# Folding eight logit columns into w_out, and native fp32 value products for eight pairs of heads instead of twelve

## The chip, the cores and the metric

The kernel runs on one core of one Trainium2 chip. The core has TensorE (PE in the rows; PEld is its loading of stationary operands), VectorE (DVE), ScalarE (ACT), GpSimd (POOL) and the queue engine SyncE (SP), which here only issues transfers. What is measured is the device time of one execution in microseconds (us). The number to predict is the median of several runs.

## The reference

Three layers follow each other, all in float32:

```python
# attention: 4 batches, 8 heads, 576 tokens, 64 columns per head
scores = q @ k.T / 8
scores = where(scores >= max(scores) - tau, scores, -1e9)
attn   = exp(scores - max) / (sum + 1e-9)
x      = (attn @ v), heads side by side          # 2304 tokens x 512
# first MoE: 512 -> 768 -> 512
h = maximum(maximum(x @ w1, x @ w2), x @ w3)
x = h @ w_out
# second MoE: one of 8 experts for each token
logits = x @ w_gate + modality_bias[modality_id]
e      = argmax(logits);  g = softmax(logits)[e]
out    = g * (relu(x @ w1[e]) @ w2[e])           # 512 -> 1024 -> 512
```

The logits are a linear function of h, since `x @ w_gate` is `h @ (w_out @ w_gate)`.

## The kernel before, in words

**Split products.** Most products of TensorE use a rounded format (F32R). Each operand is split into a high part (rounded) and a low part (the rest), and three products (high by high, high by low, low by high) are summed in a bank of PSUM. For some heads the products are made in native fp32 instead, without a split: `nat_s` pairs of heads for the scores and `nat_a` = 12 pairs for the values (`av`, L346). There are 32 pairs, in the order batch, group, pair; group 0 of a batch has 256 tokens, group 1 has 320. A value product of a native head is `m<-th,vv 128*64` in the rows; one of a split head has `128*128` and also reads `tl`, the low part of the transposed weights of attention.

**Attention tiles.** `run_tiles` (L658) goes through 144 tiles of 128 rows: four for a pair of group 0, five for a pair of group 1. For each tile, the scores of the next tile are made (`s<-kk,qh`), VectorE takes the maxima (L275) and applies the mask (L270), ScalarE takes the exponential (L295), TensorE transposes the tile before (`pt<-idn,e`), and when a head is complete its values are multiplied. A native head copies the transposed tile once (L323). A split head copies it to `pc` (L318), rounds it to `th` (L325) and subtracts to `tl` (L748, VectorE); its values are also split (L239 ScalarE, L240 GpSimd).

**First MoE as filler.** When the four pairs of a group are done, blocks of 256 tokens become ready: after tiles 16, 36, 52, 72, 88, 108 and 124 one each, and two at the end. `fill` (L400) weaves the generator `moe1` (L415) into the tiles: each tile grants 900 + 900 units, and the generator yields 440 or 430 units after a few products. A block has 18 accumulations of 12 products with 256 columns (w1, w2, w3, with the maximum on VectorE, L439), and then for each half of its tokens 18 products with 512 columns (`m<-w,hh` and `m<-w,hl`), whose sum ScalarE copies to `x1` (L465) and SyncE stores to `xd` (L466). PSUM tiles named `m` come from a pool with two banks, which values, first MoE and logits share. What is left of the blocks at the end of attention runs in `phase2`, where the banks are named `ph2`, in program order.

**Logits.** After a block, `logits` (L472) transposes each 128 tokens of x1 with four products (`m<-idn,x`), copies them to `x1t` on VectorE (L481), multiplies with `wgs` (8 columns, eight records in the trace) and adds the bias (L486). It runs as a side task of `fill`. The last block has its own version, `last_logits` (L490, L504 to L511). The routing of the second MoE reads the sums: `route_part`, `early` (which takes the most frequent expert of the first 16 token tiles as the early slot) and `final`.

**Weights.** `convert_weights` (L120) takes w1, w2, w3 and then w_out in 24 chunks of 512 columns from float64 words: a load, then one step on ScalarE (L138), three on VectorE (L139, L141, L143), a rounded copy on ScalarE (L144) and a subtraction on GpSimd (L145). `conv_step` makes at most three steps for each tile, so about one chunk a tile over the first 24 tiles; `convert` forces steps when a product needs a chunk that isn't there yet.

**Order.** The program's order is planned by the framework's timeline simulation when the kernel is built; in `phase2` TensorE's order is fixed by hand (`drive`), with due times in ns.

Of the kernel before, what the change touches and what calls it, by code (L numbers as in the profile page):

```python
# [10 lines left out]
F32 = mybir.dt.float32  # L11
F32R = mybir.dt.float32r
# [4 lines left out]
ALU = mybir.AluOpType  # L17
# [5 lines left out]
NT, DM, DFF = 2304, 512, 768  # L23
E, F2 = 8, 1024
# [8 lines left out]
G3 = 3  # L33
# [7 lines left out]
XROW = DM + 4  # L41
# [4 lines left out]
def f32(ap):  # L46
    return ap.bitcast(F32)


class Kern:  # L50
# [66 lines left out]
    def wtile(self):  # L117
        return self.wp.tile([128, WCH], F32R, name="w")

    def convert_weights(self):  # L120
        nc = self.nc
        nw = 3 * KF * KD * 128 // WCH
        self.wm = [(self.wtile(), self.wtile()) for _ in range(nw + KF * DM // WCH)]
        n = CCH
        for w, (hi, lo) in enumerate(self.wm):
            for s in range(WCH // n):
# [7 lines left out]
                hf, lf = hi[:, s * n:s * n + n], lo[:, s * n:s * n + n]  # L134
# [9 lines left out]
                nc.scalar.copy(hf, tf)  # L144
                nc.gpsimd.tensor_tensor(lf, tf, f32(hf), op=ALU.subtract)  # L145
                self.wready += n
                yield

    def w13s(self, f, m, kc):
        w, o = divmod(((f * 3 + m) * KD + kc) * 128, WCH)  # L150
        self.convert(w * WCH + o + 128)
        return [t[:, o:o + 128] for t in self.wm[w]]

    def wos(self, f):
        w, o = divmod(3 * KF * KD * 128 + f * DM, WCH)
        self.convert(w * WCH + o + DM)
        return [t[:, o:o + DM] for t in self.wm[w]]
# [257 lines left out]
    def moe1(self, i):  # L415
# [34 lines left out]
        x1s = self.x1s = []  # L450
        self.x1i = i
        for t in range(2):
            tt = 2 * i + t
            cs = slice(t * 128, t * 128 + 128)
            ps = self.psA()
            ops = []
            for f in range(KF):
                oh, ol = self.wos(f)
                ops += [(hH[f][:, cs], oh), (hL[f][:, cs], oh), (hH[f][:, cs], ol)]
            for n, (a, r) in enumerate(ops):  # L460
                self.mm(ps, lhsT=a, rhs=r, start=n == 0, stop=n == len(ops) - 1)
                if n % 2 and n < 17:
                    yield 430
            x1 = self.po.tile([128, DM], F32, name="x1")
            nc.scalar.copy(x1, ps)  # L465
            nc.sync.dma_start(self.xd[tt * 128:tt * 128 + 128, :], x1)  # L466
            x1s.append(x1)
            yield 430
        if i < NBLK - 1:
            self.side.append(self.logits(i, x1s))  # L470

    def logits(self, i, x1s):  # L472
        nc = self.nc
        for t in range(2):
            tt = 2 * i + t
            x1 = x1s[t]
            pt = self.psL()
            for kc in range(KD):
                self.tp(pt[:, kc, :], x1[:, kc * 128:kc * 128 + 128], self.idn)
            x1t = self.po.tile([128, KD, 128], F32, name="x1t", bufs=1)  # L480
            nc.vector.tensor_copy(x1t, pt)  # L481
            yield self.lag(440, 1500)
            pl = self.psL()[:, 0, :]
            for kc in range(KD):
                self.mm(pl[:, :E], lhsT=x1t[:, kc, :], rhs=self.wgs[:, kc, :], start=kc == 0, stop=kc == KD - 1)
            nc.vector.tensor_tensor(self.lg[:, tt, :], pl[:, :E], self.bias[:, tt, :], op=ALU.add)  # L486
            yield self.lag(440, 0)
        self.logged = i + 1

    def last_logits(self):  # L490
        nc = self.nc
        i = NBLK - 1
        xt = []
        pl = self.psL()
        for t in range(2):
            while len(self.x1s) <= t:
                yield 400
            yield 1100
            pt = self.psL()
            for kc in range(KD):  # L500
                self.tp(pt[:, kc, :], self.x1s[t][:, kc * 128:kc * 128 + 128], self.idn)
            xt.append(self.pa.tile([128, KD, 128], F32, name="x1t", bufs=2))
            if t:
                nc.scalar.copy(xt[t], pt)  # L504
            else:
                nc.vector.tensor_copy(xt[t], pt)
        for t in range(2):
            yield 1300 if t else 0
            for kc in range(KD):
                self.mm(pl[:, t, :E], lhsT=xt[t][:, kc, :], rhs=self.wgs[:, kc, :], start=kc == 0, stop=kc == KD - 1)  # L510
        nc.vector.tensor_tensor(self.lg[:, 2 * i:2 * i + 2, :], pl[:, :2, :E], self.bias[:, 2 * i:2 * i + 2, :], op=ALU.add)  # L511

    def phase1(self):
# [35 lines left out]
        self.conv = self.convert_weights()  # L549
# [3 lines left out]
    def phase2(self):  # L553
# [5 lines left out]
        self.psL = lambda: self.ps2.tile([128, DM], F32, name="y2p", bufs=G3).rearrange("p (a b) -> p a b", b=128)  # L559
# [6 lines left out]
                 (lambda: self.x1i == NBLK - 1, self.late_routing())]  # L566
# [140 lines left out]
    nat_a = 12  # L707
    x1s = ()
    x1i = -1
# [241 lines left out]
    def late_routing(self):  # L951


        for gen in (self.last_logits(), self.final()):
            while True:
                with self.tc.high_priority(offset=self.hot):
                    x = next(gen, None)
                if x is None:
                    break
                yield x  # L960
# [249 lines left out]
```

## Time and profile before

| | |
|---|---|
| median of 3 runs | 904.38 us (902.39 to 906.71) |
| profiled execution | 905.14 us, span 903.4 us |
| TensorE, VectorE, ScalarE, GpSimd busy | 859.1, 604.8, 565.5, 484.2 us |
| mean granted TensorE clock | 0.986 of full speed |
| attention tiles | 8.8 to about 590 us |
| first MoE | from about 68 to 682 us |
| slots of the second MoE | about 682 us to the end |

The span runs from the first to the last instruction of the profiled execution. Products are pipelined and their ends are modelled, so a busy time close to the span says that TensorE has work, not that it runs at its peak; start-to-start times tell what a product costs. The time in front of a row is its start in us, and x with a number is how many instructions the row merges.

### The profile page before, as it was taken

What the parts mean: (1) busy time and instruction counts of PE and PEld (TensorE: products, weight loads), DVE (VectorE), ACT (ScalarE), POOL (GpSimd) and SP (SyncE); (2) the same over time, 40 slices, a digit from 0 to 9 for tenths busy, and PEclk for the clock granted to TensorE, in tenths of its full rate; (3) what the DMA queues carried; (4) which work ended last, traced back from release to release, by engine and by line L of the source; (5) the groups of instructions that cost most, each with busy time, mean ns of one, the idle gap of its engine ahead of it and who ended that gap; (6) DMA issues with size and microseconds to landing.
All of it is one profiled execution on the core that took longest, in us unless ns stands there. A gap on an engine that the chain in (4) does not pass through costs nothing.

```text
span 903.4 us, 16815 instructions
## 1 busy us (share of the span) xinstructions
PE 859.1 (95%) x5616; PEld 761.9 (84%) x5616; DVE 604.8 (67%) x1425; ACT 565.5 (63%) x1167; POOL 484.2 (54%) x779
## 2 busy tenths in 40 slices
PE   7878999999999989999999999999999999999995
PEld 4546876787789979999988999989999899899894
DVE  6888984654488987887989889845475663453540
ACT  4767785665588897978998888741152353453440
POOL 5978996564576877967887877321030322121011
PEclk9988999999999999999999999999999999999998
DMA  6655652232222232332232221000050224320001
GB/s 185 173 151 151 165 151 65 80 85 60 68 74 58 79 99 60 87 94 59 74 91 73 81 86 54 9 24 1 27 220 24 71 58 152 117 71 36 1 36 37
DMA packets 58234, 74.26 MB, mean 82 GB/s; under 512 B 27424, under 2 KB 40480, under 8 KB 58144
## 3 DMA queue, kind: packets, MB, share of 16 engines
q1 hardware_dynamic: 54448, 63.66, 24.6%
q0 software_dynamic: 2880, 9.44, 3.1%
q8 instruction: 46, 0.75, 0.4%
q14 instruction: 44, 0.36, 0.1%
q10 hardware_dynamic: 816, 0.04, 0.1%
HBM read 80.46 MB, written 9.44 MB: 100 GB/s over the span
## 4 chain that ended last, share of the span: by engine, by line
PE 53%; issue 20%; DVE 8%; POOL 7%; ACT 6%; DMA 5%; SPq 0%; POOLq 0%; ACTq 0%; DVEq 0%
PE m L69 29%; PE ph L69 9%; PE s L69 6%; PE pt L72 4%; PE y2p L69 2%; POOL out L1153 2%; POOL kk L232 1%; DVE e L270 1%; DVE mx L275 1%; POOL xg L1075 1%; DVE tl L748 1%; PE p L72 1%; DMA tl<-w 1%; ACT e L295 1%; DMA qr<-q 1%
## 5 line engine op out<-in xcount | busy, mean ns | idle before, releaser
L69 PE MATMUL m<-xh,w 128*128 128x256 f32 x1008 | 202.3, 290 | 1.4 <-ACT xh L392 1.0
L69 PEld LDWEIGHTS m<-xh,w 128*128 128x128 f32 x1008 | 162.7, 192 | 5.3 <-issue 2.6
L69 PE MATMUL m<-xl,w 128*128 128x256 f32 x504 | 144.5, 287 | 2.4 <-POOL xl L393 2.3
L69 PE MATMUL m<-th,vv 128*64 128x256 f32 (+5 forms) x440 | 130.9, 381 | 8.7 <-ACT th L323 3.8
L270 DVE SCALAR_TENSOR_TENSOR e<-s,mx,e 128x576 f32<-128x576 f32 x144 | 116.8, 812 | 30.7 <-ACT e L295 29.0
L275 DVE TENSOR_REDUCE mx<-s 128x1 f32<-128x576 f32 x144 | 106.6, 750 | 33.8 <-PE s L69 32.9
L295 ACT ACTIVATE e<-s,mx 128x576 f32<-128x576 f32 x144 | 106.9, 743 | 17.4 <-DVE mx L275 12.6
L69 PE MATMUL ph<-x2h,w 128*128 128x384 f32 x384 | 103.8, 342 | 0.0
L69 PEld LDWEIGHTS m<-th,vv 128*64 128x64 f32 (+2 forms) x440 | 69.2, 167 | 39.5 <-issue 14.5
L69 PE MATMUL y2p<-w 128*128 128x512 f32 x432 | 100.5, 391 | 0.0
L69 PEld LDWEIGHTS m<-xl,w 128*128 128x128 f32 x504 | 96.5, 192 | 3.7 <-POOL xl L393 3.1
L69 PE MATMUL s<-kk,qh 128*128 128x288 f32 (+1 forms) x272 | 88.8, 357 | 11.3 <-DMA kk<-k 5.7
L232 POOL TENSOR_TENSOR kk<-kr,kk 64x576 fp32r<-64x576 f32 x60 | 90.3, 1505 | 16.3 <-ACT kk L231 6.4
L72 PE MATMUL pt<-idn,e 128*128 128x128 f32 x576 | 91.0, 279 | 6.4 <-ACT th L323 6.3
L69 PEld LDWEIGHTS y2p<-w 128*128 128x128 f32 x432 | 80.7, 188 | 16.3
L748 DVE TENSOR_TENSOR tl<-pc,th 128x512 fp32r<-128x512 f32 (+1 forms) x104 | 82.2, 798 | 10.4 <-ACT th L325 9.7
L1129 DVE SCALAR_TENSOR_TENSOR w<-ph,w 128x384 fp32r<-128x384 f32 x48 | 26.7, 556 | 82.7 <-ACT w L1128 82.5
L72 PEld LDWEIGHTS pt<-idn,e 128*128 128x128 f32 x576 | 69.9, 144 | 13.6 <-ACT th L323 8.8
L444 POOL TENSOR_TENSOR hl<-hacc,hh 128x256 fp32r<-128x256 f32 x54 | 44.1, 818 | 58.5 <-ACT hh L443 52.8
L69 PEld LDWEIGHTS s<-kk,qh 128*128 128x128 f32 (+1 forms) x272 | 53.6, 199 | 21.7 <-issue 9.2
L69 PEld LDWEIGHTS ph<-x2h,w 128*128 128x128 f32 x384 | 70.2, 188 | 0.2
L279 POOL TENSOR_SCALAR mx<-mx 128x1 f32<-128x1 f32 x144 | 40.9, 284 | 52.1 <-DVE e L270 36.8
(226 smaller groups left out, 2005.0 us busy)
## 6 DMA issues: line engine op xcount, KB each, us to landing
r<-w SPq DMA_DIRECT2D x48, 512.0 KB
kr<-k SPq DMA_DIRECT2D x120, 144.0 KB
tl<-w SPq DMA_DIRECT2D x18, 512.0 KB
qr<-q SPq DMA_DIRECT2D x120, 64.0 KB
vr<-v SPq DMA_DIRECT2D x40, 160.0 KB
xd<-x SPq DMA_DIRECT2D x18, 256.0 KB
vv<-v SPq DMA_DIRECT2D x24, 160.0 KB
tl<-wo SPq DMA_DIRECT2D x6, 512.0 KB
```

Of the source, the lines that this page charges most:

```text
L69: return self.pin(self.nc.tensor.matmul(*args, **kw))
L72: return self.pin(self.nc.tensor.transpose(*args, **kw))
L232: nc.gpsimd.tensor_tensor(kk[64:128], kr[64:128], f32(kk[64:128]), op=ALU.subtract)
L270: self.conv_step(v.scalar_tensor_tensor(e, sv, mx[:, 1:2], e, op0=ALU.is_ge, op1=ALU.mult, accum_out=mx[:, 2:3]))
L275: self.conv_step(v.tensor_reduce(mn[:, 0:1], sn, axis=AX.XY, op=ALU.max, negate=True))
L279: nc.gpsimd.tensor_scalar(mx[:, 3:4], mx[:, 2:3], 1e-9, None, op0=ALU.add)
L295: nc.scalar.activation(e, sv, AF.Exp, bias=mx[:, 0:1], scale=1.0)
L444: nc.gpsimd.tensor_tensor(l, acc[f], f32(h), op=ALU.subtract)
L748: nc.vector.tensor_tensor(l, src, f32(h), op=ALU.subtract)
L1075: self.nc.gpsimd.indirect_dma_start(out=xg, out_offset=None, in_=sl["src"], in_offset=bass.IndirectOffsetOnAxis(ap=sl["gidx"][:, g:g + 1], ...
L1129: nc.vector.scalar_tensor_tensor(h[:, SLOT:2 * SLOT], ph, 0.0, f32(h[:, :SLOT]), op0=ALU.max, op1=ALU.subtract)
L1153: nc.gpsimd.indirect_dma_start(out=sl["out"][g], out_offset=bass.IndirectOffsetOnAxis(ap=sl["sidx"][:, g:g + 1], axis=0), in_=y, in_offset ...
```

## The change

The eight columns of w_out times w_gate are made once, from the converted w_out, and stand beside the columns of w_out: each half of the token tile's output is then a product of 256 + 8 columns and one of 256. The eight columns of the sum get the bias and are the logits. `logits` and `last_logits` go away. For this, w_out is converted first and w1, w2, w3 after it, and each of the six chunks of w_out is transposed and multiplied with w_gate in two further steps (`gate_columns`) while the next chunk is converted. `moe1` yields 440 after four products and 220 after each half. The routing of the last block begins when its logits are there. Separately, `nat_a` becomes 8: pairs 8 to 11 (batch 1, group 0) use split value products.

```diff
--- before.py
+++ after.py
@@ -38,7 +38,8 @@
 NC = KF2 // 2
 NK = 6
 WBUF = 24
-XROW = DM + 4
+HALF = DM // 2
+ROW = DM + E
 WCH = 1024
 CCH = 512
 
@@ -114,15 +115,24 @@
 
         self.xd = self.ctx.enter_context(tc.tile_pool(name="dram", bufs=1, space=DRAM)).tile([NT, DM], F32, name="xd")
 
-    def wtile(self):
-        return self.wp.tile([128, WCH], F32R, name="w")
+    def wtile(self, full=False):
+        w = self.wp.tile([128, 2 * ROW], F32R, name="w")
+        return w if full else w[:, :WCH]
+
+    def conversion(self):
+        for _ in self.convert_weights():
+            if self.gates and next(self.gates[0], self) is self:
+                self.gates.pop(0)
+            yield
 
     def convert_weights(self):
         nc = self.nc
         nw = 3 * KF * KD * 128 // WCH
-        self.wm = [(self.wtile(), self.wtile()) for _ in range(nw + KF * DM // WCH)]
+        self.wm = [(self.wtile(w >= nw), self.wtile(w >= nw)) for w in range(nw + KF * DM // WCH)]
         n = CCH
-        for w, (hi, lo) in enumerate(self.wm):
+
+        for w in [*range(nw, len(self.wm)), *range(nw)]:
+            hi, lo = self.wm[w]
             for s in range(WCH // n):
                 src, c0 = (self.w13, w) if w < nw else (self.wo, w - nw)
                 c0 = c0 * WCH + s * n
@@ -131,7 +141,6 @@
                 t = self.po.tile([128, n], F32, name="x1").bitcast(U32)
                 nc.sync.dma_start(raw, src[:, c0:c0 + n].bitcast(U32).rearrange("p (c two) -> p c two", two=2))
                 h, l = raw[:, :, 1], raw[:, :, 0]
-                hf, lf = hi[:, s * n:s * n + n], lo[:, s * n:s * n + n]
                 tf = t.bitcast(F32)
 
 
@@ -141,20 +150,45 @@
                 nc.vector.scalar_tensor_tensor(t, h, 0x80000000, t, op0=ALU.bitwise_and, op1=ALU.bitwise_or)
                 yield
                 nc.vector.scalar_tensor_tensor(t, l, 29, t, op0=ALU.logical_shift_right, op1=ALU.bitwise_or)
-                nc.scalar.copy(hf, tf)
-                nc.gpsimd.tensor_tensor(lf, tf, f32(hf), op=ALU.subtract)
+                if w < nw:
+                    parts = [(s * n, 0, n)]
+                else:
+                    parts = [(s * ROW, 0, HALF), (s * ROW + HALF + E, HALF, HALF)]
+                for o, i, m in parts:
+                    hf = hi[:, o:o + m]
+                    nc.scalar.copy(hf, tf[:, i:i + m])
+                    nc.gpsimd.tensor_tensor(lo[:, o:o + m], tf[:, i:i + m], f32(hf), op=ALU.subtract)
+                if w >= nw:
+                    o = s * ROW + HALF
+                    self.gates.append(self.gate_columns(tf, hi[:, o:o + E], lo[:, o:o + E]))
                 self.wready += n
                 yield
 
+    def gate_columns(self, w, hi, lo):
+
+        nc = self.nc
+        yield
+        pt = self.psL()
+        for kc in range(KD):
+            self.tp(pt[:, kc, :], w[:, kc * 128:kc * 128 + 128], self.idn)
+        wt = self.pe.tile([128, 4, 128], F32, name="pc", bufs=2)
+        nc.scalar.copy(wt, pt)
+        yield
+        pl = self.psL()[:, 0, :E]
+        for kc in range(KD):
+            self.mm(pl, lhsT=wt[:, kc, :], rhs=self.wgs[:, kc, :], start=kc == 0, stop=kc == KD - 1)
+        self.split_out(hi, lo, pl)
+
     def w13s(self, f, m, kc):
         w, o = divmod(((f * 3 + m) * KD + kc) * 128, WCH)
-        self.convert(w * WCH + o + 128)
+        self.convert(KF * DM + w * WCH + o + 128)
         return [t[:, o:o + 128] for t in self.wm[w]]
 
     def wos(self, f):
-        w, o = divmod(3 * KF * KD * 128 + f * DM, WCH)
-        self.convert(w * WCH + o + DM)
-        return [t[:, o:o + DM] for t in self.wm[w]]
+
+        w = (3 * KF * KD * 128 + f * DM) // WCH
+        o = f % 2 * ROW
+        return [[t[:, a:b] for t in self.wm[w]] for a, b in ((o, o + HALF + E), (o + HALF + E, o + ROW))]
 
     def convert(self, n):
         while self.wready < n:
@@ -447,68 +481,27 @@
             if i == NBLK - 1 and self.eslot and n0 >= 6:
                 self.weights(n0 // 2)
             yield 440
-        x1s = self.x1s = []
-        self.x1i = i
         for t in range(2):
             tt = 2 * i + t
             cs = slice(t * 128, t * 128 + 128)
-            ps = self.psA()
-            ops = []
-            for f in range(KF):
-                oh, ol = self.wos(f)
-                ops += [(hH[f][:, cs], oh), (hL[f][:, cs], oh), (hH[f][:, cs], ol)]
-            for n, (a, r) in enumerate(ops):
-                self.mm(ps, lhsT=a, rhs=r, start=n == 0, stop=n == len(ops) - 1)
-                if n % 2 and n < 17:
-                    yield 430
             x1 = self.po.tile([128, DM], F32, name="x1")
-            nc.scalar.copy(x1, ps)
+            for d in range(2):
+                n = HALF + E * (1 - d)
+                ps = self.psA()[:, :n]
+                ops = []
+                for f in range(KF):
+                    oh, ol = self.wos(f)[d]
+                    ops += [(hH[f][:, cs], oh), (hL[f][:, cs], oh), (hH[f][:, cs], ol)]
+                for n, (a, r) in enumerate(ops):
+                    self.mm(ps, lhsT=a, rhs=r, start=n == 0, stop=n == len(ops) - 1)
+                    if n % 4 == 3:
+                        yield 440
+                nc.scalar.copy(x1[:, d * HALF:d * HALF + HALF], ps[:, :HALF])
+                if d == 0:
+                    nc.vector.tensor_tensor(self.lg[:, tt, :], ps[:, HALF:], self.bias[:, tt, :], op=ALU.add)
+                yield 220
             nc.sync.dma_start(self.xd[tt * 128:tt * 128 + 128, :], x1)
-            x1s.append(x1)
-            yield 430
-        if i < NBLK - 1:
-            self.side.append(self.logits(i, x1s))
-
-    def logits(self, i, x1s):
...
         self.logged = i + 1
-
-    def last_logits(self):
...
     def phase1(self):
         tc = self.tc
@@ -546,7 +539,8 @@
         self.ph = opn(p1, "ph", 1)
         self.po = opn(p1, "po", 2)
         self.wready = 0
-        self.conv = self.convert_weights()
+        self.gates = []
+        self.conv = self.conversion()
         self.run_tiles(heads, tiles)
         at.close()
 
@@ -556,14 +550,13 @@
         self.pa = opn(ctx, "p2a", 1, side="right")
         self.ps2 = opn(ctx, "ps2", 1, PSUM, side="right")
         self.raw = tuple(self.pa.tile([128, NC, WCH], F32, name=n) for n in ("r1", "r2"))
-        self.psL = lambda: self.ps2.tile([128, DM], F32, name="y2p", bufs=G3).rearrange("p (a b) -> p a b", b=128)
         self.psA = lambda: self.ps2.tile([128, 512], F32, name="ph2", bufs=3)
         self.outs = dram_disjoint_views(self.out, (NSTAT + 2) * G3)
         self.route_tiles()
         self.pinned = True
         self.slots = []
         parts = [(lambda: self.logged >= 7, self.route_part(0, 14)), (lambda: self.logged >= 8, self.early()),
-                 (lambda: self.x1i == NBLK - 1, self.late_routing())]
+                 (lambda: self.logged >= NBLK, self.late_routing())]
         self.drive(self.main(), parts)
         n = nc.values_load(self.eT[0:1, NTL:], min_val=NSTAT * G3, max_val=NTL)
         with tc.For_i(NSTAT * G3, n, G3) as i:
@@ -704,9 +697,7 @@
             self.prepped += 1
 
     nat_s = 2
-    nat_a = 12
-    x1s = ()
-    x1i = -1
+    nat_a = 8
     eslot = None
     conv_rate = (1, 1)
     conv_credit = 0
@@ -950,14 +941,13 @@
 
     def late_routing(self):
 
-
-        for gen in (self.last_logits(), self.final()):
-            while True:
-                with self.tc.high_priority(offset=self.hot):
-                    x = next(gen, None)
-                if x is None:
-                    break
-                yield x
+        gen = self.final()
+        while True:
+            with self.tc.high_priority(offset=self.hot):
+                x = next(gen, None)
+            if x is None:
+                break
+            yield x
 
     def final(self):
```

## Rows read from the trace of the kernel before

**Rows 1.** The page, busy time, share of the span and instructions.
```profile
PE 859.1 (95%) x5616; PEld 761.9 (84%) x5616; DVE 604.8 (67%) x1425; ACT 565.5 (63%) x1167; POOL 484.2 (54%) x779
```

**Rows 2.** Stages: length, PE, PEld, DVE, ACT, POOL busy, clock, DMA, GB/s.
```profile
0.00:100.00 100.00, 81.59 (x366) 52.40 (x367) 82.06 (x177) 68.93 (x135) 77.64 (x125) 0.93 0.59 163
...
162.50:231.00 68.50, 67.07 (x452) 54.15 (x451) 34.46 (x98) 43.17 (x97) 39.52 (x76) 1.00 0.27 70
...
375.40:515.00 139.60, 135.87 (x1016) 129.60 (x1015) 119.42 (x289) 118.31 (x263) 107.78 (x180) 0.99 0.28 78
...
600.00:727.00 127.00, 126.17 (x902) 118.51 (x901) 67.80 (x226) 36.58 (x68) 25.11 (x32) 1.00 0.19 67
```

**Rows 3.** TensorE's waits, 130 to 600 us: total, times, longest.
```profile
PE s L69 <- DVE e L270: 4.1, 6, 1.4
...
PE m L69 <- DVE x1t L481: 1.7, 2, 1.2
...
PE m L69 <- ACT xh L392: 0.2, 1, 0.2
```

**Rows 4.** Timeline of TensorE: first MoE, 256 columns (start, busy us).
```profile
578.82 0.40 PE L69 MATMUL m<-xh,w 128*128 128x256 f32 x2
579.06 0.28 PE L69 MATMUL m<-xl,w 128*128 128x256 f32 x1
```

**Rows 5.** Timeline of TensorE: w_out, 512 columns.
```profile
680.52 0.39 PE L69 MATMUL ph<-w,hl 128*128 128x512 f32 x1
680.75 0.61 PE L69 MATMUL ph<-w,hh 128*128 128x512 f32 x2
681.20 0.39 PE L69 MATMUL ph<-w,hl 128*128 128x512 f32 x1
```

**Rows 6.** Timeline of all engines: the last logits.
```profile
681.43 0.39 PE L69 MATMUL ph<-w,hh 128*128 128x512 f32 x1
...
683.25 0.60 PE L72 MATMUL y2p<-idn,x 128*128 128x128 f32 x4
683.68 0.96 PE L69 MATMUL y2p<-wgs,x1t 128*128 128x8 f32 x8
...
684.49 0.42 PE L69 MATMUL ph<-x2h,w 128*128 128x384 f32 x1
...
687.15 0.17 DVE L511 TENSOR_TENSOR bias<-y2p,bias 128x16 f32<-128x16 f32 x1 [0.77 <-PE y2p L69]
```

**Rows 7.** Timeline of TensorE: native values of one head.
```profile
201.52 2.51 PE L69 MATMUL m<-th,vv 128*64 128x256 f32 x10
203.96 0.40 PE L69 MATMUL s<-kk,qh 128*128 128x288 f32 x1
```

**Rows 8.** Groups by line, 313.5 to 375.4 us: busy, mean ns, idle before.
```profile
L748 DVE TENSOR_TENSOR tl<-pc,th 128x512 fp32r<-128x512 f32 x16 | 14.6, 918 | 1.2 <-ACT th L325 1.2
...
L318 ACT COPY pc<-pt 128x512 f32<-128x512 f32 x16 | 9.4, 585 | 0.5 <-DVE mx L275 0.4
...
L240 POOL TENSOR_TENSOR vv<-vr,vv 128x320 fp32r<-128x320 f32 x7 | 6.2, 881 | 1.8 <-ACT vv L239 1.5
...
L239 ACT CAST vv<-vr 128x320 fp32r<-128x320 f32 x8 | 3.7, 459 | 0.1
```

**Rows 9.** Timeline of ScalarE: exponentials of tiles 34, 36, 52, 72, 88.
```profile
159.16 0.75 ACT L295 ACTIVATE e<-s,mx 128x576 f32<-128x576 f32 x1
...
163.70 0.76 ACT L295 ACTIVATE e<-s,mx 128x576 f32<-128x576 f32 x1
...
230.96 0.74 ACT L295 ACTIVATE e<-s,mx 128x576 f32<-128x576 f32 x1
...
313.51 0.74 ACT L295 ACTIVATE e<-s,mx 128x576 f32<-128x576 f32 x1
...
375.40 0.74 ACT L295 ACTIVATE e<-s,mx 128x576 f32<-128x576 f32 x1
```

**Rows 10.** Groups by line, whole span: weight loads of the w_out products.
```profile
L69 PEld LDWEIGHTS m<-w,hh 128*128 128x128 f32 x156 | 29.1, 188 | 6.6 <-ACT remh L248 0.5 <-issue 0.4 <-DVE hacc L439 0.3
```

More of the change, by code (lines that the diff above doesn't have):

```diff
@@ L465, in moe1 @@
-            nc.scalar.copy(x1, ps)
-            nc.sync.dma_start(self.xd[tt * 128:tt * 128 + 128, :], x1)
-            x1s.append(x1)
-            yield 430
-        if i < NBLK - 1:
-            self.side.append(self.logits(i, x1s))
-    def logits(self, i, x1s):
[L473 to L487, printed above, removed]
-        self.logged = i + 1
@@ L490, in last_logits @@
-    def last_logits(self):
[L491 to L511, printed above, removed]
+            x1 = self.po.tile([128, DM], F32, name="x1")
```

## The prediction

> **What bounds the kernel now.** I read the page first: TensorE is busy for 859 of 903 us, VectorE for 605, ScalarE for 566, GpSimd for 484 [rows 1]. An average hides stages, so I split the span next [rows 2]. In the first 100 us VectorE is the fullest (82.1, against 81.6 of TensorE with a granted clock of 0.93): this is where the weights are converted. In the stretches shown from 162 to 515 us TensorE is at 97 to 98%, but VectorE and ScalarE are near 85% from 375 to 515 us; from 600 to 727 us TensorE has 126.2 of 127 us and the others little. Busy TensorE counts modelled ends, so I took the waits as a check: between 130 and 600 us the twelve groups of its waits sum to 14 us, the largest 4.1 us on VectorE's mask, and 1.7 us on the copy x1t of the logits [rows 3]. So after 130 us TensorE's stream sets the pace, and the change is to be priced in start-to-start times of products, not in their durations (a 256-column product lasts 0.28 us, but two start within 0.24 us).
>
> **Price of a column.** 256 columns: (579.06 - 578.82)/2 = 0.120 us from start to start [rows 4]. 512 columns: (681.20 - 680.52)/3 = 0.227 us [rows 5]. On the line between them 264 columns take 0.120 + 8 x 0.107/256 = 0.123 us.
>
> **The change part by part.**
>
> *The logits' own products go.* For each of 18 token tiles four transposes (683.25 to 683.68, 0.43 us) and eight product records with wgs (683.68 to 684.49, 0.81 us) go, 1.24 us [rows 6]: 18 x 1.24 = -22.3 us, 12 tiles (14.9 us) before 600 us and 6 (7.4 us) after. What TensorE waited for x1t goes too: -1.7 us [rows 3]. VectorE loses the copies x1t; its bias add stays.
>
> *w_out in two halves.* Each 512-column product becomes one of 264 and one of 256: 0.123 + 0.120 - 0.227 = +0.016 us; 9 blocks x 36 = 324 products: +5.3 us. Each half has its own weight load. That is in the prices, since the 256-column stream has a load for each product too. The Trainium skill puts it otherwise (TensorE: Matmul & The Clock Gate, Back-to-back issue gap): in a stream of load and product pairs it gives some 81 ns at 128 columns and 131 ns at 512; by that, drawn as a line, a half costs 98 ns and a pair 65 ns more than the whole, 21 us in all and not 5.3. The trace's 227 ns for 512 columns does not agree with it, so the rows decide.
>
> *Evacuation.* ScalarE copies two halves instead of 512 columns, and VectorE adds the eight logit columns from the same bank. That bank, one of two named m, now waits for both engines. The next half gives 18 x 0.12 = 2.2 us of cover in the other bank; VectorE's longest queue item is 0.8 us. I cost it at nothing; if VectorE lags by 3 us, it is 0.8 us for each of 18 tiles, 14 us.
>
> *Weights: w_out first, and gate columns.* Six chunks gain 4 transposes and 8 product records each: 6 x 1.24 = 7.4 us of TensorE, all in the first 100 us, where it has idle time and VectorE is the fullest [rows 2]. For VectorE it is six subtractions of 8 columns. GpSimd and ScalarE get two halves for one chunk, plus a copy of 512 columns on ScalarE. These are fractions of a microsecond a chunk on engines that the row of that stage shows less full than VectorE. New is a wait: the transposes wait for the converted chunk, and behind them on TensorE's queue stand the next tile's scores, for which VectorE's maxima wait. From 0 to +7.4 us (all products in the open); I take +2, since the chunk was finished one step earlier. That w13 comes six chunks later is hidden: the first block begins at tile 16, one chunk is converted for each tile, so ten are there, and the block needs about 1.4 for each tile and 18 in all; it never catches up.
>
> *Values of pairs 8 to 11.* A head's native product is 10 records in 2.44 us (201.52 to 203.96) [rows 7]; split it is 9 products of 256 columns, 1.08 us. Eight heads: at most -10.9 us. In exchange each head brings two copies pc (0.59 us) and one vv cast (0.46) to ScalarE, two tl of 0.92 us to VectorE, one vv of 0.88 us to GpSimd [rows 8]. There is room: in these tiles (162.5 to 231.0) VectorE is busy for 34 of 68 us, ScalarE for 43 [rows 2]. The best yardstick is the same kind of group that already runs split: 16 tiles took 230.96 - 163.70 = 67.3 us native, 375.40 - 313.51 = 61.9 us split, with the same grant to the first MoE for each [rows 9]. I take the difference, -5.4 us, which holds the new side work; bounds -10.9 and 0.
>
> *The filler budget.* Each tile grants 1800 to the first MoE. A block asked for 9 x 2640 + 2 x 3870 and 1760 for its logits, 33260; it will ask for 23760 + 2 x 3960 = 31680, so 17.6 tiles and not 18.5. Blocks become ready at fixed tiles (16, 36, 52, 72, 88, 108, 124). Before, only the first block ran out before the next was ready (tiles 34.5 to 36); after, four do, for 2.4 + 0.8 + 0.8 + 0.8 = 4.8 tiles, 3.3 more. The filler's part of a tile is 1800/31680 of a block's 216 x 0.120 + 72 x 0.122 = 34.7 us, 2.0 us. If a dry tile takes as long as a full one (67.3/16 = 4.2 us), these 2.0 us of TensorE are lost, 6.5 us in all. Tiles 34 and 35 took (163.70 - 159.16)/2 = 2.3 us each [rows 9], the full time less 1.9, by which nothing is lost. Two tiles are few, and each starts when the planned order lets it; I take the middle, +3. The rest of block 6 (18 products) moves ahead of 600 us, which is neutral where TensorE is full.
>
> *The end of the routing.* The last w_out product starts at 681.43 us and the last logits are added at 687.15 [rows 6]; after the change the add follows the product, some 5 us earlier. But the early slot's products cover the routing in any case: TensorE has work for 126.2 of 127 us there [rows 2]. Nothing gained.
>
> **Sum.** -22.3 - 1.7 + 5.3 + 2 - 5.4 + 3 = -19.1 us. The profiled execution took 905.1 us (its span 903.4), 0.7 over the median of 904.4: 905.1 - 19.1 - 0.7 = 885 us. The order of the instructions is planned anew, which no row prices; the range takes it.
>
> **Rivals.**
>
> *More lands.* The split values give all 10.9 us and dry tiles run faster: 905.1 - 22.3 - 1.7 + 5.3 + 2 - 10.9 = 877.5, range 870 to 880. For it: TensorE is the fullest in all those stages. Against: ScalarE, 43 us now and 8 x (2 x 0.59 + 0.46) = 13 us more, reaches 56/62 = 90% in pairs 8 to 11.
>
> *Half lands before 600 us.* VectorE and ScalarE, at 85%, take over the pace: 7.4 + 7.4 of the logits, 3 of the values: 905.1 - 14.8 - 3 + 5.3 + 2 + 3 = 898; range 891 to 900.
>
> *Nothing lands before 600 us.* Only 7.4 us less 72 x 0.016 = 1.2 after it: 905.1 - 6.2 + 2 + 3 = 904, no change. Against: the waits of [rows 3].
>
> *Slower: gate products in the way early.* Place: the first ten tiles, 12 stops (transposes, then products, six times) at the head of TensorE's queue, each waiting on VectorE's conversion or a free bank m. The other terms give 21 us, so from 21/12 = 1.8 us a stop the gain is gone, and from 2.2 us it is slower by 0.5%; at 3 us, 919. For it: VectorE is full there and three conversion steps lie between load and result. Against: TensorE has 18 idle us in that stage.
>
> *Slower: a load for each half stands in the open.* 324 more loads of some 0.188 us [rows 10] would be 61 us: 941. The 256-column stream with a load for each product at 0.120 us [rows 4] speaks against it. The skill's pace of pairs named above would give 901 instead, and the traces so far refute it at 512 columns.
>
> **Chances.** Forecast (880 to 891) 0.52; more 0.20; half 0.13; nothing 0.08; gate products 0.05; loads 0.02. A measurement here tells about 0.5% (4.5 us) from no change. Faster by more: the first two and most of the third, 0.83. Within: nothing, and the rest of half, 0.10. Slower: 0.07. The range takes in more and half: 871 to 899; it leaves out the last three cases and the edges.
>
> **What would show it.** Between 150 and 600 us no product with wgs and no copy x1t, and two halves starting 0.24 us apart together. The 16 tiles of pairs 8 to 11 in 62 us rather than 67, with ScalarE near 90%. The first 36 tiles ending (the exponential of tile 36) within 3 us of 163.7. Stretches without first-MoE products before tiles 36, 72, 108 and 144. From the end of attention to the first second-layer product of the early slot, some 10 us less, of which 4 are only moved. I am wrong if tiles 0 to 36 take over 5 us more, if TensorE waits on bank m (its releaser a VectorE bias or ScalarE copy) for over 5 us, or if pairs 8 to 11 keep their 67 us.

## The result and the profile after

The changed kernel takes 894.69 us (median of four runs, 889.62 to 895.52) against 903.76 us for the kernel before; the ratio is 0.987 (95% interval 0.9839 to 0.99). So it is faster by 1.3%, by 9 us and not by the 19 that I forecast. The profiled run took 895.52 us with a span of 893.7 us.

First the page, busy time by engine, as in [rows 1], and then the four stages of [rows 2], the middle two moved to where their tiles now stand (the second is now exactly tiles 36 to 52):

```profile
PE 842.5 (94%) x5788; PEld 766.4 (86%) x5788; DVE 609.8 (68%) x1447; ACT 580.0 (65%) x1226; POOL 492.3 (55%) x793
```

```profile
0.00:100.00 100.00, 79.77 (x320) 53.80 (x321) 68.48 (x150) 60.36 (x127) 64.32 (x114) 0.89 0.55 148
180.06:244.31 64.25, 59.22 (x453) 53.70 (x452) 47.73 (x118) 51.32 (x112) 48.19 (x79) 1.00 0.28 78
391.60:531.00 139.40, 134.85 (x1084) 131.35 (x1084) 117.77 (x291) 122.11 (x274) 108.61 (x186) 1.00 0.29 84
600.00:727.00 127.00, 125.92 (x957) 120.78 (x956) 71.63 (x235) 40.03 (x77) 28.71 (x34) 1.00 0.20 71
```

TensorE is busy for 17 us less in all, yet in the first 100 us every engine does less than before: VectorE, the fullest there, fell from 82 to 68 us. It isn't relieved; it waits. The exponentials of tiles 4, 16, 36, 52, 72 and 88 on ScalarE, the counterpart of [rows 9], show what that costs:

```profile
21.88 0.75 ACT L329 ACTIVATE e<-s,mx 128x576 f32<-128x576 f32 x1
88.83 0.74 ACT L329 ACTIVATE e<-s,mx 128x576 f32<-128x576 f32 x1
180.06 0.74 ACT L329 ACTIVATE e<-s,mx 128x576 f32<-128x576 f32 x1 [0.16 <-DVE mx L314]
244.31 0.72 ACT L329 ACTIVATE e<-s,mx 128x576 f32<-128x576 f32 x1
317.44 0.75 ACT L329 ACTIVATE e<-s,mx 128x576 f32<-128x576 f32 x1
383.46 0.75 ACT L329 ACTIVATE e<-s,mx 128x576 f32<-128x576 f32 x1
```

Cut at such exponentials, the two profiled spans differ like this (us):

| stretch | before | after | difference |
|---|---|---|---|
| start to tile 36 | 163.7 | 180.1 | +16.4 |
| tiles 36 to 52 (pairs 8 to 11) | 67.3 | 64.2 | -3.1 |
| tiles 52 to 143 | 357.3 | 342.3 | -15.0 |
| tile 143 to the end | 315.1 | 307.1 | -8.0 |

After tile 36 the change gives 26 us; the first 36 tiles take 16 of them back, 13 of these between tiles 4 and 16 (54.0 us before, 67.0 after).

**How they are lost.** Tiles 4 to 16, before and after, in the columns of [rows 2] (TensorE is the first busy time, VectorE the third):

```profile
20.76:74.80 54.04, 44.37 (x195) 26.41 (x194) 46.85 (x95) 40.02 (x79) 45.29 (x61) 0.91 0.58 162
```

```profile
21.88:88.83 66.95, 55.42 (x234) 37.95 (x232) 46.45 (x100) 42.99 (x95) 46.46 (x68) 0.85 0.47 132
```

VectorE has as much work as before, 46 us. TensorE is busy for 11 us more, but its idle time does not shrink: 9.7 us before, 11.5 after. The gate products, busy for 13.2 us there, were not taken up by the idle time; they came on top of it. Two places in those twelve tiles show how VectorE is kept waiting. Here is TensorE, then VectorE, around the first:

```profile
32.96 1.87 PE L70 MATMUL m<-wgs,pc 128*128 128x8 f32 x8
34.77 4.72 PE L70 MATMUL m<-th,vv 128*64 128x256 f32 x10
39.42 1.00 PE L73 MATMUL pt<-idn,e 128*128 128x128 f32 x4
40.39 0.38 PE L70 MATMUL s<-kk,qh 128*128 128x288 f32 x1
40.61 0.29 PE L70 MATMUL s<-kk,ql 128*128 128x288 f32 x1
```

```profile
36.10 0.17 DVE L334 TENSOR_TENSOR w<-m,w 128x8 fp32r<-128x8 f32 x1 [0.22 <-ACT w L333]
41.21 0.76 DVE L309 TENSOR_REDUCE mx<-s 128x1 f32<-128x576 f32 x1 [4.95 <-PE s L70]
```

A gate product, a head's native values and transposes run for 7.4 us ahead of the scores, and VectorE stands for 4.95 us. Besides, TensorE is at half its pace: the ten records take 4.72 us here and 2.51 us in [rows 7] (the last section tells how to read its clock there). At the second place VectorE itself is the cause:

```profile
70.43 0.82 DVE L304 SCALAR_TENSOR_TENSOR e<-s,mx,e 128x576 f32<-128x576 f32 x1 [0.30 <-ACT e L329]
...
74.74 0.43 DVE L148 TENSOR_SCALAR x<-x 128x512 uint32<-128x512 uint32 x1 [3.48 <-ACT x L147]
...
78.27 0.69 DVE L152 SCALAR_TENSOR_TENSOR x<-tl,x 128x512 uint32<-128x512 uint32 x1
78.88 0.75 DVE L309 TENSOR_REDUCE mx<-s 128x1 f32<-128x576 f32 x1
```

```profile
73.34 0.29 PE L70 MATMUL s<-kk,ql 128*128 128x288 f32 x1
```

```profile
73.97 0.66 ACT L147 ACTIVATE x<-tl 128x512 f32<-128x512 f32 x1 [2.76 <-DMA tl<-w]
```

The scores were done at 73.6 us, but their maxima stand in VectorE's queue behind two conversions, the first of which waits for ScalarE, which waits for a chunk's load; TensorE then has next to nothing to do until 81 us (0.34 us of work from 76 to 80). No gate product stands here: the last of them ended at 61 us. VectorE's waits for scores in tiles 4 to 16 add up to 10.8 us.

### The profile page after: what moved, and what is told of

It reads as the page before. It is cut to its first block, busy times and chain, and to the rows that moved or that the text cites. A ratio compares the mean times of both kernels' runs of the same rounds, so it can differ in the third digit from the quotient of the medians.

```text
span 893.7 us, 17267 instructions
## 1 busy us (share of the span) xinstructions
PE 842.5 (94%) x5788; PEld 766.4 (86%) x5788; DVE 609.8 (68%) x1447; ACT 580.0 (65%) x1226; POOL 492.3 (55%) x793
## 4 chain that ended last, share of the span: by engine, by line
PE 57%; issue 19%; POOL 8%; ACT 6%; DMA 5%; DVE 4%; SPq 1%; POOLq 0%; ACTq 0%; DVEq 0%
PE m L70 31%; PE ph L70 10%; PE s L70 7%; PE pt L73 5%; DMA kr<-k 3%; PE y2p L70 2%; POOL out L1143 2%; POOL kk L266 2%; POOL xg L1065 1%; PE p L73 1%; DMA tl<-w 1%; ACT e L329 1%; ACT kk L265 1%; DVE tl L739 1%; DVE mx L309 1%
## 5 line engine op out<-in xcount | busy, mean ns | idle before, releaser
L70 PE MATMUL m<-xh,w 128*128 128x256 f32 x1008 | 199.5, 287 | 6.0 <-DVE xf L406 2.1
L70 PEld LDWEIGHTS m<-xh,w 128*128 128x128 f32 x1008 | 160.6, 188 | 10.2 <-DVE xf L406 2.9
L304 DVE SCALAR_TENSOR_TENSOR e<-s,mx,e 128x576 f32<-128x576 f32 x144 | 116.5, 812 | 27.8 <-ACT e L329 26.1
L70 PE MATMUL m<-th,vv 128*128 128x320 f32 (+5 forms) x400 | 117.8, 365 | 0.3 <-DVE xf L406 0.3
L70 PE MATMUL s<-kk,qh 128*128 128x288 f32 (+1 forms) x272 | 92.7, 372 | 16.4 <-DVE e L304 11.0
L739 DVE TENSOR_TENSOR tl<-pc,th 128x512 fp32r<-128x512 f32 (+1 forms) x120 | 94.3, 791 | 14.3 <-ACT th L359 13.5
L266 POOL TENSOR_TENSOR kk<-kr,kk 64x576 fp32r<-64x576 f32 x60 | 88.0, 1467 | 16.1 <-ACT kk L265 5.9
L70 PEld LDWEIGHTS m<-th,vv 128*128 128x128 f32 (+2 forms) x400 | 66.6, 173 | 22.9 <-issue 11.6
L70 PEld LDWEIGHTS s<-kk,qh 128*128 128x128 f32 (+1 forms) x272 | 55.6, 208 | 26.5 <-DVE e L304 12.2
L1143 POOL DMA_INDIRECT out<-y,f_sidx x15 | 15.0, 997 | 100.1 <-ACT y L1142 99.7
```

Source lines behind the costliest of these rows:

```text
L70: return self.pin(self.nc.tensor.matmul(*args, **kw))
L266: nc.gpsimd.tensor_tensor(kk[64:128], kr[64:128], f32(kk[64:128]), op=ALU.subtract)
L304: self.conv_step(v.scalar_tensor_tensor(e, sv, mx[:, 1:2], e, op0=ALU.is_ge, op1=ALU.mult, accum_out=mx[:, 2:3]))
L739: nc.vector.tensor_tensor(l, src, f32(h), op=ALU.subtract)
L1143: nc.gpsimd.indirect_dma_start(out=sl["out"][g], out_offset=bass.IndirectOffsetOnAxis(ap=sl["sidx"][:, g:g + 1], axis=0), in_=y, in_offset ...
```

## The experiments

### Each half of the change alone

```diff
# e1_values, from the kernel before
-    nat_a = 12
+    nat_a = 8
# e2_logits, from the changed kernel
-    nat_a = 8
+    nat_a = 12
```

> The kernel before with only the values changed (8 pairs native instead of 12). Theory G (the gate products in the first tiles cost the missing 16 us) and theory O (w_out converted first costs them): nothing changes before tile 36, whose exponential stays at 163.7 +- 2 us; pairs 8 to 11 (tiles 36 to 52) go from 67.3 to 62 us; total 898 to 900. Theory P (any newly planned order of the first tiles moves them by some 10 us either way): tile 36 moves by more than 5 us.

> The changed kernel with 12 pairs native again, so the logits' part alone. Theories G and O: tile 36 at 180 +- 3 us as in the changed kernel, tiles 36 to 52 at 67 us, total 898 to 900. Theory P: tile 36 anywhere from 165 to 190.

The values alone: 899.12 us (ratio 0.9924, 0.9892 to 0.9956); pairs 8 to 11 took 63.1 us instead of 67.3, and tile 36 came at 163.2, so a new plan by itself does not move it. The logits' columns alone: 905.04 us, ratio 1.0006 (0.9974 to 1.0037), with tile 36 at 176.2; that is 5 us over the 898 to 900 expected. So the values give 4 to 6 us by themselves, and the half that removes 22 us of products gains nothing while it keeps the loss of the first 36 tiles. The two ratios do not add up to the 0.987 of both together; why, no run here tells.

### Is it the order of the conversions, or the amount of gate work?

```diff
# e8_order, from the kernel before
-        for w, (hi, lo) in enumerate(self.wm):
+        for w in [*range(nw, len(self.wm)), *range(nw)]:
+            hi, lo = self.wm[w]
...
-        self.convert(w * WCH + o + 128)
+        self.convert(KF * DM + w * WCH + o + 128)
...
-        self.convert(w * WCH + o + DM)
# e5_double, from the changed kernel
-                    self.gates.append(self.gate_columns(tf, hi[:, o:o + E], lo[:, o:o + E]))
+                    self.gates += [self.gate_columns(tf, hi[:, o:o + E], lo[:, o:o + E]) for _ in range(2)]
```

> The kernel before with w_out converted first and nothing else. Theory O: tile 36 at 175 us or later, total 912 or more. Theory G: tile 36 at 162 to 166 us, total 900 to 907.

> The changed kernel with each chunk's gate columns made twice, the second over the first, same result. To be read up to tile 36 (180 us in the changed kernel, 164 before). Theory G (gate products in the first tiles cost the 16 us): 190 to 200 us. Theory O (the order of the conversions costs them): 180 to 185 us.

Converting w_out first costs nothing: 904.33 us in one run, tile 36 at 160.9. With twice the gate work tile 36 comes at 182.1 and not at 190 or later; that is the range of theory O, which e8 rules out. The one run took 900.86 us. The 182.1 hides two parts: tiles 4 to 16, where the loss sits, took 59.8 us, less than the 67.0 with the gate work made once, and 18.4 us went in tile 34, where TensorE worked off the first block. So, by one run each, neither the order nor the amount is the price, and a price per stop does not hold either: in tiles 4 to 16 there are 21 stops for 11.

### The gate work elsewhere

```diff
# e3_wo_last: w13 converted first, gates with w_out's chunks (in the trace: tiles 24 to 29)
-        for w in [*range(nw, len(self.wm)), *range(nw)]:
+        for w in range(len(self.wm)):
...
+        self.convert(3 * KF * KD * 128 + KF * DM)
+        while self.gates:
+            next(self.conv)
# e4_gates_late: all gates after the last conversion (in the trace: tiles 29 to 34), the chunk summed again on GpSimd
-            if self.gates and next(self.gates[0], self) is self:
+            yield
+        while self.gates:
+            if next(self.gates[0], self) is self:
...
+        w = self.po.tile([128, DM], F32, name="x1")
+        for a, b in ((0, 0), (HALF, HALF + E)):
+            nc.gpsimd.tensor_tensor(w[:, a:a + HALF], f32(hi[:, o + b:o + b + HALF]), f32(lo[:, o + b:o + b + HALF]), op=ALU.add)
# e7_delay: the same sum, but from the seventh chunk on, two and three steps apart
+            if self.gates and self.wready > 6 * CCH:
```

> The changed kernel with w_out converted last, as before the change, so that its gate products run at tiles 18 to 26, among the first MoE's products. Theories G and O: tile 16 is back at 75 us (89 in the changed kernel); the gate products cost their 7.4 us later; total 884 to 889. Theory P: no gain that is certain, total 890 to 900.

> The changed kernel, w_out still converted first, but its gate columns made after the last conversion (tiles 24 to 29), from a sum of the high and low parts on GpSimd. Theory G: tile 16 is back at 75 us, total 884 to 889. Theory O: tile 16 stays at 88 us or more, total 895 to 903.

> The changed kernel with the gate products at tiles 7 to 19, long after their chunks are converted (the chunk is summed again from its two parts on GpSimd) and each step two or three conversion steps after the one before. Theory G by waits: tile 36 at 165 to 171 us, total 880 to 887. Theory G by work: tile 36 at 176 to 184 us, total 892 to 898.

All three missed. e3: 909.18 us (ratio 1.0048, 1.002 to 1.0075). Tiles 0 to 24 are no slower than before, but 24 to 36 take 87.2 us instead of 54.2. Two stops of TensorE in that stall, and then the stages view of its worst 20 us:

```profile
112.54 1.11 PE L73 MATMUL m<-idn,x 128*128 128x128 f32 x4 [2.20 <-DVE x L156]
116.03 1.87 PE L70 MATMUL m<-wgs,pc 128*128 128x8 f32 x8 [2.37 <-ACT pc L179]
```

```profile
100.00:120.00 20.00, 10.67 (x44) 8.69 (x43) 16.95 (x31) 10.95 (x24) 16.97 (x23) 0.59 0.49 148
```

From 100 to 120 us TensorE has 10.67 us of work, at a granted clock of 0.59. This is the rival "gate products in the way" in the open: 2.2 to 2.4 us a stop, once on VectorE's conversion step and once on ScalarE's copy. These two are a part of the loss only: tile 36 comes 28 us later than before the change, and 16 of them are idle time of TensorE. e4: 914.57 us (ratio 1.0116, 1.006 to 1.0172), 83.5 us for tiles 24 to 36; there TensorE waits for the sum on GpSimd (4.7 us on it, 4.3 in one piece). e7: 898.5 us (ratio 0.9936, 0.9911 to 0.9961), tile 36 at 175.1 where 165 to 171 was expected; its sum on GpSimd is work that the changed kernel does not have.

### Taking the wait away

```diff
# e6_free
-            self.tp(pt[:, kc, :], w[:, kc * 128:kc * 128 + 128], self.idn)
+            self.tp(pt[:, kc, :], self.idn, self.idn)
# e9_apart: converted chunks of w_out in buffers of their own, gate steps 4 and 3 steps apart
-                t = self.po.tile([128, n], F32, name="x1").bitcast(U32)
+                if w < nw:
+                    t = self.po.tile([128, n], F32, name="x1").bitcast(U32)
+                else:
+                    if s == 0:
+                        keep = self.px.tile([128, KD, BLK], F32R, name="xl" if w == nw + 1 else "xh").rearrange("p a b -> p (a b)")
+                    t = keep[:, s * n:s * n + n].bitcast(U32)
...
         yield
+        yield
+        yield
+        yield
         pt = self.psL()
...
         yield
+        yield
+        yield
         pl = self.psL()[:, 0, :E]
# e10_rate: three conversion steps for four
-    conv_rate = (1, 1)
+    conv_rate = (0.75, 1)
```

> The changed kernel with as many gate products at the same places, but their transposes read the constant identity and not the converted chunk, so the logits are others and the experts' slots too: to be read only up to tile 36. Theory G by waits (TensorE's queue stands still until the chunk is converted): 165 to 171 us. Theory G by work (the products' own TensorE time, longer at the lower clock, and their copies): 176 to 184 us. Theory O: 176 to 184 us.

> The changed kernel with the converted w_out kept in buffers of its own, so that a chunk's transposes stand four conversion steps behind its conversion and its products three steps behind its transposes, with no other work added. Theory W (the cost is TensorE standing at gate products whose chunk or copy isn't ready): tile 36 at 164 to 171 us, total 880 to 888. Theory L (any gate product in the first tiles lengthens the chain of a tile, ready or not, and each new plan scatters the conversions): tile 36 at 172 to 182 us, total 889 to 898.

> The changed kernel with three quarters of the conversion steps in the first 16 tiles. Theory W: the products wait as before, tile 36 at 176 to 184 us, total 891 to 899. Theory L, in the form that conversions crowd the chain of the first tiles: tile 16 earlier than 84 us (88.8 in the changed kernel), tile 36 at 165 to 174 us.

e6 computes other logits and so another routing; only its first 36 tiles are read: tile 36 at 168.7, within the 165 to 171 expected of waits. But its gate products do not stand at the same places: with nothing to wait for, the first ones came at 1.6 and 4.5 us (19.3 and 24.5 in the changed kernel), so e6 takes away more than the wait. e9 hit, by theory W: **882.36 us** (881.27 to 884.52), ratio 0.9751 (0.9706 to 0.9796), tile 36 at 164.2. It is the fastest version of all. e10 speaks against W in turn, with tile 16 at 75.0, and went beyond theory L: 887.94 us, ratio 0.9805 (0.9761 to 0.9849), tile 36 at 163.1. That last mark flatters it: 54 of the first block's 72 w_out products, 6.5 us at 0.12 us each, are still to come there, and tiles 36 to 52 take 69.4 us. So the loss of tiles 4 to 16 goes when the gate products stand further from the conversions, and also when the conversions are thinner.

### Which part of it, and both together

e6, e9 and e10 all also ease the ring x1 of two buffers, which the gate transposes hold while the next conversions want it.

```diff
# e11_kept: the own buffers of e9_apart without its spacing
# e12_both: e9_apart with
-    conv_rate = (1, 1)
+    conv_rate = (0.75, 1)
```

> The changed kernel, with the converted chunks of w_out in buffers of their own, so that the gate transposes hold no buffer of the ring x1 that the next-but-one chunk's conversion needs; the gate steps stand where they stand in the changed kernel. Theory R (the ring: a conversion waits on ScalarE until TensorE has transposed the chunk before the last): all of the loss goes, the exponential of tile 36 comes at 163 to 170 us and the median is 880 to 888 us. Theory S (TensorE stands with products that aren't ready yet at the head of its queue, and the next scores behind them): little goes, tile 36 comes at 175 to 182 us and the median is 890 to 897 us. In between, both count, in the proportion of tile 36 between 164 and 180 us.

> The version with the gate steps apart and own buffers, and conversions spread over the tiles at 0.75 of the pace as well. If the two cure one and the same loss: no more than either alone, tile 36 at 162 to 166 us and a median of 880 to 887 us. If the bunched conversions cost something of their own beside the gate products: tile 36 at 156 to 161 us and a median of 874 to 880 us.

e11: 892.99 us (888.28 to 895.03), ratio 0.9868 (0.9826 to 0.991), tile 36 at 179.0: theory R (the ring) falls, S fits, and the spacing alone makes the difference between e11 and e9. But e12 missed both forms: 891.17 us (886.48 to 894.27), tile 36 at 176.9, most of the loss back. Two cures that each work do not work together, so "distance from the conversions" is not the whole rule. What holds over all of them is the symptom, VectorE waiting for scores. Tiles 4 to 16 took 54.0 us before, 53.3 in e9 and 53.6 in e10, against 67.0 in the changed kernel, 65.8 in e11 and 63.0 in e12. VectorE's waits for scores in those tiles, in the changed kernel, e11, e12, e9 and e10 in this order (total, times, longest):

```profile
DVE mx L309 <- PE s L70: 10.8, 5, 4.9
```

```profile
DVE mx L314 <- PE s L70: 8.0, 6, 2.4
```

```profile
DVE mx L319 <- PE s L70: 10.5, 5, 3.4
```

```profile
DVE mx L319 <- PE s L70: 4.3, 4, 1.5
```

```profile
DVE mx L309 <- PE s L70: 4.6, 4, 2.8
```

The slow ones wait 8 to 11 us, the fast ones 4 to 5. In e9 TensorE's queue shows the good order, scores first and the gate product behind them:

```profile
56.11 1.94 PE L70 MATMUL m<-th,vv 128*64 128x256 f32 x8
57.98 0.40 PE L70 MATMUL s<-kk,qh 128*128 128x288 f32 x1
58.22 0.29 PE L70 MATMUL s<-kk,ql 128*128 128x288 f32 x1
58.35 0.29 PE L70 MATMUL s<-kk,qh 128*128 128x288 f32 x1
58.48 0.29 PE L70 MATMUL s<-kk,ql 128*128 128x288 f32 x1
58.61 0.95 PE L70 MATMUL m<-wgs,pc 128*128 128x8 f32 x8
```

In e12 the same gate work is spaced just as far, yet here eight records of values at half pace (the granted clock is 0.50 there) and the gate transposes precede the scores, and the maxima wait 3.41 us for them (TensorE):

```profile
68.88 3.67 PE L70 MATMUL m<-th,vv 128*64 128x256 f32 x8
72.48 1.11 PE L73 MATMUL m<-idn,xl 128*128 128x128 f32 x4
73.53 0.80 PE L70 MATMUL m<-th,vv 64*64 64x256 f32 x2
74.26 0.33 PE L73 MATMUL p<-idn,e 128*128 128x128 f32 x1
74.34 0.38 PE L70 MATMUL s<-kk,qh 128*128 128x288 f32 x1
```

A second thing goes with the loss in all fourteen traces, the time that TensorE spends at its lower clock (us, tiles 4 to 16; up to a trace's first clock entry it counts as lower, see the last section):

| kernel | tiles 4 to 16 | VectorE waits for scores | TensorE at 0.50 |
|---|---|---|---|
| before | 54.0 | 1.4 | 14.7 |
| e9, e10 | 53.3, 53.6 | 4.3, 4.6 | 12.1, 15.9 |
| e1, e3, e4, e6, e8 | 50.7 to 54.6 | 0.4 to 5.3 | 5.9 to 18.0 |
| e2, e5, e7 | 59.8 to 63.8 | 6.3 to 8.5 | 20.2 to 28.8 |
| e12 | 63.0 | 10.5 | 22.7 |
| e11 | 65.8 | 8.0 | 32.8 |
| changed | 67.0 | 10.8 | 38.8 |

The five kernels without gate products in these tiles (before, e1, e3, e4, e8) are all fast, whatever their plan; of the nine with them six are slow. So the loss needs gate products there, and whether it comes differs from one order to the next. The planner makes a new order for every variant, and what stands between two tiles' scores comes out of it. In the rows of e9 and of e12 a head's values stand ahead of the scores (eight records, 1.94 us in e9 and 3.67 in e12). Why the planner puts the gate work ahead of them as well in e12 and behind them in e9, no run here tells; that stays open.

## Why the prediction came out as it did

**The mis-sized term: gate columns early, +2 with bounds 0 and +7.4.** It measured +16.4 us by tile 36, over twice the upper bound, and so one of the prediction's own signs of being wrong came true (tiles 0 to 36 over 5 us slower). The bound was the products' own time, as if the worst were that all of it stood in the open. Even that was priced too low: it came from [rows 6], where TensorE runs at its full clock, and in the first tiles many run at half; the twelve groups of gate products last 14.3 us together, 9.3 by the shortest group of each kind. The rival named the place and the wait (things that stand ahead of the next scores, on which VectorE depends), and its condition came out close: 16.4 us over 12 stops is 1.4 us each, below the 1.8 from which the gain would be gone. I gave it 0.05, because TensorE had 18 idle us in that stage. That was the wrong row to argue from: the work did not go into the idle time, which is 9.7 us of tiles 4 to 16 before and 11.5 after. e5 shows that a price for each stop was still the wrong form: with ten more stops the tiles 4 to 16 ran faster, not slower.

The other part that the term left out is TensorE's pace. It is at the lower clock for 14.7 us of these tiles before and for 38.8 after: its first rise comes at 40.2 us and not at 25.2, and from 52 to 64 us the granted clock is 0.50, the 1.2 GHz level, after four microseconds (48 to 52) in which TensorE had 2.93 us of work. I summed, over tiles 4 to 16, what each group of products lasted beyond the shortest group of the same shape and count in the same trace: some 7 us before, 14 to 15 after, 7 in e9. So, as an estimate, about 7 of the 13 us between those tiles come from products that ran slower. The Trainium skill (TensorE: Matmul & The Clock Gate, What's actually happening) makes the slow level the engine's default, which activity releases. The traces agree in that all fourteen begin at the slow level. Whether the gaps came first or the slow products did, and why the first rise comes 15 us later, the traces don't say.

**Logits' products, -22.3, halves +5.3, wait -1.7.** Right in direction. A half of 264 columns starts every (165.61 - 163.68)/16 = 0.121 us and one of 256 every (172.51 - 170.62)/16 = 0.118 us, so two halves are 0.24 us as predicted, and a pair costs 0.012 us over a whole, not 0.016. TensorE's timeline, the second and the last product of each run of 18:

```profile
163.68 0.28 PE L70 MATMUL m<-w,hl 128*128 128x264 f32 x1
...
165.61 0.29 PE L70 MATMUL m<-w,hh 128*128 128x264 f32 x1
...
170.62 0.28 PE L70 MATMUL m<-w,hl 128*128 128x256 f32 x1
...
172.51 0.28 PE L70 MATMUL m<-w,hh 128*128 128x256 f32 x1
```

The rival of loads in the open is out, and so is the Trainium skill's pace of load and product pairs, as the prediction cites it. These three terms make -18.7 us, with 16 of the 18 token tiles after tile 52; the trace shows -23.0 from there on, -15.0 and -8.0. More than the sign can't be read from that: the ten kernels with the same products after tile 52 (e6 left out for its routing) take 649.3 us (the changed kernel, the shortest) to 657.4 there, for 672.4 before.

**Values of pairs 8 to 11, -5.4.** The stretch fell by 4.2 us alone (e1), 3.1 with the logits and 6.6 in e9. It also moves without them: with native values it took 65.9 us in e2 and 64.5 in e8. ScalarE reached 51.3 of 64.25 us, 80% and not the 90% forecast, and TensorE has 5 us free there, so the pace is no longer TensorE's alone (59.2 us busy, where [rows 2] shows 67.1 of 68.5).

**Evacuation, 0.** Right, though VectorE's longest item in [rows 8] is 0.92 us and not 0.8: from 146 to 600 us TensorE waited for VectorE's bias on bank m once, 0.3 us; its largest group there is another (total, times, longest):

```profile
PE pt L73 <- ACT pc L352: 3.6, 5, 1.3
...
PE m L70 <- DVE bias L501: 0.3, 1, 0.3
```

**Filler budget, +3.** Mostly not seen. In TensorE's timeline one stretch without first-MoE products ends tile 35 (178.4 to 183.3 us) and one of 8.2 us follows in tiles 36 to 38 (184.7 to 192.9), where the kernel before had 12.5 and 6.4 us; from 193 to 590 us the only one above 4.5 us (5.4, from 328.3) lies in tiles 75 to 76, and none ahead of tiles 72, 108 or 144, where I had them. The sum after tile 36 is -26.1 us; mine without the gate columns was -21.1, this +3 in it, and about 1 us of that falls before tile 36.

**The end of the routing, 0.** From tile 143's exponential to the first second-layer product of the early slot it took 113.2 us (588.29 to 701.52) and now takes 104.5 (586.6 to 691.12): 8.7 us less, where I wrote some 10. The last logits now come before the last half of w_out is done, on VectorE and TensorE:

```profile
672.01 0.17 DVE L501 TENSOR_TENSOR bias<-ph,bias 128x8 f32<-128x8 f32 x1 [4.15 <-ACT x L499]
```

```profile
673.43 0.28 PE L70 MATMUL ph<-w,hh 128*128 128x256 f32 x1
```

The time lay inside the whole range (871 to 899), not in the forecast's band (880 to 891), and that is luck: two errors partly cancel, 16.4 us lost where I had 2, and 5 to 6 us more gained after tile 36 than my sum. It fell into the band of "half lands" (891 to 900), but not for that rival's reason, which was that the gain before 600 us goes to VectorE and ScalarE: tiles 52 to 143 gave 15.0 us. With the loss cured, e9 shows what the rest is worth: 24 us of its own profiled run against the 905.14 of the one before, where my terms without the gate columns give 21.

## What to carry to other kernels

Where two engines hand a tile to each other, idle time on one is not room: what is put on it ahead of the hand-over can come on top of the cycle, and more so if the engine's pace drops. Price such an insert by what is queued behind it and who waits for that, and at the clock of the place where it will stand, not by its duration elsewhere; and try it a few steps later before giving it up: here five `yield`s and buffers of their own were worth some 11 us. And when a planner orders the instructions, measure each variant; two cures that work alone need not add up.

## What was not expected of the hardware

The granted clock of a stretch can read 1.00 while TensorE runs at half pace. In the changed kernel's trace it does so up to 40 us. A group of four gate transposes takes 1.09 us there and 0.60 us right behind; two stretches, then TensorE's rows:

```profile
36.00:40.00 4.00, 4.00 (x11) 1.80 (x10) 0.17 (x1) 0.43 (x3) 2.50 (x4) 1.00 0.59 182
40.00:44.00 4.00, 4.00 (x24) 2.59 (x22) 2.60 (x7) 2.53 (x5) 0.21 (x1) 1.00 0.34 75
```

```profile
26.25 1.09 PE L73 MATMUL m<-idn,x 128*128 128x128 f32 x4
...
41.01 0.60 PE L73 MATMUL m<-idn,x 128*128 128x128 f32 x4
```

The 1.00 is no measurement: the clock entries of this trace begin at 40.2 us, and time without an entry counts as full. In all fourteen traces the first entry, between 22.6 and 40.2 us, is a full one, and four transposes ahead of it take 1.06 to 1.12 us. So that column, with the 0.93 of [rows 2], is too high in the first stage; durations of a known shape tell more there.

The run time goes mostly with the mean granted clock of the run. The changed kernel took 889.62 us at 0.991, 894.24 at 0.981 and 895.15 at 0.979, though 895.52 at 0.983; e11 took 888.28 at 0.990 and 895.03 at 0.979. At 0.991 one run of e9 took 881.27 us, 8 us less than the changed kernel's run at that clock.
